# A spectral filter with a soft mixture of experts: the x step with its constant as weights, signs per row, constants in slot 4, and the read-backs of batches 1 and 2 a slot sooner

## The chip, the cores and the metric

The kernel runs on one core of a Trainium2 chip. The metric is device time in microseconds (us) of one execution, the median of the runs taken. The core's engines work side by side and wait for each other through semaphores: TensorE (PE, with the weight loads PEld beside it), VectorE (DVE), ScalarE (ACT), GpSimd (POOL), and SyncE (SP), whose queue issues most of the transfers.

## The reference

```python
X = np.fft.rfft(x, axis=1)                    # x: (8, 2496, 256)
y = np.fft.irfft(X * (filt_r + 1j * filt_i)[None], n=2496, axis=1)
x = y.reshape(19968, 256)
logits = x @ phi                              # phi: (256, 32), 8 experts of 4 slots
d = np.exp(logits - logits.max(0)); d /= d.sum(0) + 1e-09      # over the tokens
slot_input = (d.T @ x).reshape(8, 4, 256)
for e in range(8):                            # w1: (8, 256, 1024), w2: (8, 1024, 256)
    slot_out[e] = np.maximum(slot_input[e] @ w1[e], 0.0) @ w2[e]
c = np.exp(logits - logits.max(1)); c /= c.sum(1) + 1e-09      # over the 32 slots
return c @ slot_out                           # (19968, 256)
```

All of it is in float32.

## The kernel before

**The transform.** 2496 = 39 * 64, so the Fourier transform of a batch goes in two stages. The first, over 39 points, is done for batch 0 by `first_stage` (L407) and for each later batch by `s1_unit` (step s, L356, four matmuls a piece, each in a 64*64 tile of the array). It leaves 20 rows t (`NT`) of the half spectrum. The second, over 64 points, is `x_unit` (step x, L434); it takes two rows t, a pair, at a time. So a batch has ten pairs (`CPB`), and the eight batches make 80 **slots** of the main loop, slot n working on pair `divmod(n, 10)`. What batches 1 to 7 leave in the first stage, `at`, is copied out by ACT, stored in device memory (`a_dram<-at`, by `store_a`), and read back in the other order (`ash<-a_dram`, by `load_ash`); batch 0 is turned on the chip instead (`turn`).

**One slot.** `x_unit(n)` makes four products with `ash` as the weights (128 rows, 128 columns) and the constant `a1` or `b0` (128 columns) as the operand that streams. The result has the 256 channels on the partitions, in two halves. DVE multiplies it with the filter's table `ff_t`: `t2` by the imaginary part, `part` by the real one; then an addition and a subtraction give the filtered pair `yt`, on DVE in batches 0 to 5, on POOL from batch 6 on (`PA = 6`). Step t (`t_unit`, L467) works on the pair of two slots before (`LT = 2`): four transposes of 128 by 128 and a copy by ACT to `y`, where rows are on the partitions. In every second slot step l (L485), eight matmuls in 128*32 tiles with `phi_t` as the weights, makes the logits from `yt`.

**Around it.** `fold_x` (POOL) adds and subtracts two halves of a piece of x for `s1_unit`; pieces are loaded by `load_x` into six buffers (`XB = 6`), the next one as one is folded (`split_next`). `slot_of(b, u)` is the slot in which piece u of batch b is worked on; the last piece of batch 1 has slot 6, that of batch 2 slot 15. `load_to` reads a batch back no sooner than three slots behind the last piece. `chain(g)` holds the inverse transform's way back and the softmax sums for the groups (0, 1), (2, 3), (4, 5), (6), (7) of batches; its matmuls are called through `pe_m` (L515; transposes L512), in steps named ltr, v, lg, u, u2, dd, s, of which two are taken in each slot (`hop_slot`). For the last two groups the table `TAIL` says behind the slots which step follows which, by names such as `u2_5` (step u2 from row 5 on, `TG` rows at a time). Behind them come the experts (h, o) and the output blocks (out, L1087).

**The order.** SP issues its transfers in the order of the program. On PE a scheduler orders the instructions, held by `not_before` and by priorities. The list `held` keeps the instructions that are named there: `held[0]` the last of x, `held[1]` of s, `held[2]` of l. `keep_warm` (L313) runs matmuls on zeros before the first data is there; `make_signs` (L755) then spreads the signs of `sgn` over 128 partitions with 20 matmuls, and `sign_tables` multiplies the imaginary tables with them, two on DVE, the rest on POOL. The constants lie in `cst_t`; columns up to `NEAR` are loaded at the start, `NEAR:FAR` (426 KB) in slot 14.

Of the kernel before, what the change touches and what calls it, by code (L numbers as in the profile page):

```python
# [18 lines left out]
N1, N2 = 39, 64  # L19
# [46 lines left out]
TAIL = (  # L66
# [3 lines left out]
)  # L70
# [18 lines left out]
def shape_constants():  # L89
# [29 lines left out]
    def put(name, a):  # L119
        blocks.append((name, a))  # L120
# [19 lines left out]
    put("id", np.eye(P))  # L140
    put("sgn", sgn.reshape(NT // 2, P))
    put("m0", inverse(bh))
# [38 lines left out]
def filter_layout(filt):  # L181

    idx = np.array([[freq_of(t, c) for c in range(N2)] for t in range(NT)])
    a = filt[np.minimum(idx, SEQ - idx)]
    a = np.ascontiguousarray(a.reshape(NT, N2, 2, P).transpose(3, 0, 2, 1))
    return a.reshape(P, NT // 2, 256)

# [65 lines left out]
def fft_soft_moe(ctx, tc, x0, w0, x, ff, phi, wx, cst, w1q, out):  # L253
# [67 lines left out]
    eos = {}  # L321
    held = [None, None, None, None, None]

# [103 lines left out]
    def x_unit(b, c):  # L427

        t0 = 2 * c
        ash = ashs.pop((b, c))  # L430
        ps = ps_x.tile([P, 4, 2, 64], F32, tag="x", name=f"x_{b}_{c}")
        for k in range(2):
            for dh in range(2):
                ins = pe.matmul(  # L434
                    ps[:, 2 * k + dh].rearrange("q r c -> q (r c)"),
                    ash[:, k, dh * P : (dh + 1) * P],
                    C("a1" if t0 + k else "b0"),
                    start=True,
                    stop=True,
                )  # L440
# [7 lines left out]
        frv, fiv = (  # L448
            ff_t[:, c, k].rearrange("q (p o c) -> q p o c", o=1, c=64).broadcast_to([P, 4, 2, 64]) for k in range(2)
        )  # L450
        t2 = prod.tile([P, 4, 2, 64], F32, tag="t2", name=f"t2_{b}_{c}")
        if c % 2 == 0:
            yts[b, c // 2] = prod.tile([P, 2, 4, 2, 64], F32, tag="yt", name=f"yt_{b}_{c}")
        yt = yts[b, c // 2][:, c % 2]
        dve.tensor_tensor(out=t2, in0=ps[:, :, ::-1, :], in1=fiv, op=ALU.mult)  # L455
        add, part = (pool_e, yt) if b >= PA else (dve, ps)
        dve.tensor_tensor(out=part, in0=ps, in1=frv, op=ALU.mult)  # L457
        add.tensor_tensor(out=yt[:, :, 1, :], in0=part[:, :, 1, :], in1=t2[:, :, 1, :], op=ALU.add)  # L458
        add.tensor_tensor(out=yt[:, :, 0, :], in0=part[:, :, 0, :], in1=t2[:, :, 0, :], op=ALU.subtract)  # L459

    def t_unit(b, c):

        yt = yts[b, c // 2]
        pt = ps_t.tile([P, 2, 2, P], F32, tag="t", name=f"t_{b}_{c}")
        for k in range(2):
            for dh in range(2):
                pe.transpose(pt[:, k, dh, :], yt[:, c % 2, 2 * k + dh].rearrange("q r c -> q (r c)"), ident)  # L467
        k = (b * CPB + c) % YB - CPB
        if 0 <= k < CPB:
            if k == 0 and b * CPB + c < NS - CPB:  # L470
                big[0] = ypool.tile([P, CPB, 2, DIM], F32, tag="yb", name=f"yb_{b}_{c}", bufs=1)
            y = big[0][:, k]
        else:
            y = ypool.tile([P, 2, DIM], F32, tag="y", name=f"y_{b}_{c}")
        act.copy(y, pt.rearrange("k p h d -> k p (h d)"))  # L475
        ys[b, c] = y
        if c % 2 == 1:
            i = c // 2
            if i == 0:
                lts[b] = work.tile([P, 5, P], F32, tag="lt", name=f"lt_{b}", bufs=2)  # L480
            pl = ps_t.tile([P, P], F32, tag="t", name=f"l_{b}_{i}")
            with tc.high_priority():
                for dh in range(2):
                    for j in range(4):
                        ins = pe.matmul(  # L485
                            pl[32 * j : 32 * j + 32, :],
                            phi_t[:, dh, :],
                            yt[:, j // 2, 2 * (j % 2) + dh].rearrange("q r c -> q (r c)"),
                            start=(dh == 0),
                            stop=(dh == 1),  # L490
                        )
                        if j + dh == 0:
                            not_before(ins, held[1])
            held[2] = ins
            act.copy(lts[b][:, i, :], pl)  # L495

# [20 lines left out]
    def chain(g):  # L517
# [111 lines left out]
        for a0 in range(0, NH, 4):  # L629
# [21 lines left out]
            yield f"u{a0}"  # L651
        TG = SA if nb == 2 else HT // 2
        ended = [None, None]
# [38 lines left out]
        pss = psum([P, DIM], f"s_{g}")  # L692
        terms = [(ti, th, b2) for ti in range(HT) for th in range(2) for b2 in range(nb)]
        step = 4 * nb
        for k, (ti, th, b2) in enumerate(terms):
            j = k % 4
            t = th * HT + ti
            pe_m(
                pss[32 * j : 32 * j + 32, :],
                dd[:, ti, th, b2, :],  # L700
                ys[bs[b2], t // 2][:, t % 2, :],
                start=(k < 4),
                stop=(k >= len(terms) - 4),
            )
            if k % step == step - 1:
                yield f"s{k // step}"
# [40 lines left out]

    signs = []

    def make_signs(c0):  # L750
        n = min(4, NT // 2 - c0)
        ps = ps_c.tile([P, 4, 2, 1, N2], F32, tag="c", name=f"sgn_{c0}")
        for c in range(n):
            one = ident[:, c0 + c : c0 + c + 1].broadcast_to([P, P])
            behind("pe", pe.matmul(ps[:, c].rearrange("q k o c -> q (k o c)"), one, sgn_t, start=True, stop=True))  # L755
        sg = ypool.tile([P, 4, 2, 1, N2], F32, tag="y", name=f"sg_{c0}")
        act.copy(sg[:, 0:n], ps[:, 0:n])
        signs.append(sg)

    def sign_tables(c):  # L760
        if c >= CPB:
            return
        fi = ff_t[:, c, 1].rearrange("q (k h c) -> q k h c", k=2, h=2)
        sg = signs[c // 4][:, c % 4]
        (dve if c < 2 else pool_e).tensor_tensor(out=fi, in0=fi, in1=sg.broadcast_to([P, 2, 2, N2]), op=ALU.mult)

# [122 lines left out]
    for n in range(NS + LT):  # L889
        if n < NS:  # L890
            load_to(n)
            if n == CPB + 4:
                issue(cst_t[:, NEAR:FAR], cst[:, NEAR:FAR])
            if n == NS - 2 * CPB:
                behind("sp", sp.dma_start(cst_t[:, FAR:], cst[:, FAR:]))
            split_next(n + 1)
            store_a()
            x_unit(*divmod(n, CPB))
            sign_tables(n + 2)
            if n + 2 < CPB:  # L900
                turn(n + 2)
# [235 lines left out]
```

## Time and profile before

| | |
|---|---|
| Median of 3 runs | 379.02 us (378.91 to 382.27) |
| Profiled execution | 379.5 us, of which the span from its first to its last instruction is 377.7 us |
| Mean granted TensorE clock | 0.958 |
| PE, DVE, ACT, POOL busy | 350.9, 256.6, 175.4, 148.9 us |
| DMA | 103.92 MB, 275 GB/s on average |

An instruction's group in the profile is named by its line (L434 is line 434 of the kernel above), its engine, and what it writes and reads (`x<-cst_t,ash`). Behind "PE" a form such as 128*64 gives the rows and columns of the weights, and 128x256 the partitions and elements of the operand that streams. PE's timeline merges neighbours of one form into a row, with its start, its length and the number of instructions (x8). An fp32 matmul is two instructions, a transpose one. Matmuls overlap, so the length of a row is longer than the time to the next row's start.

### The profile page before, as it was taken

Reading aid. Unit: us, or ns where it says so; the run is one execution under the profiler, and the core shown is the slowest. Engines: PE = TensorE matmul, PEld = TensorE weight load, DVE = VectorE, ACT = ScalarE, POOL = GpSimd, SP = SyncE. Lnnn points to the kernel's source line nnn. Section 1 sums busy time; section 2 is a strip of 40 time slices with the busy share of each in tenths; the row PEclk is TensorE's granted clock in tenths of the full one; section 3 lists DMA queues with packets and bytes.
Section 4 is the critical chain, followed back from the end, with each engine's and each line's share of the span. In section 5 each row is a group of like instructions: output and inputs, shape, how many; then the busy total and the mean of one; then the engine's idle time right before and its main releaser. Section 6 shows DMA issues by size and latency. Waiting matters only on the chain.

```text
span 377.7 us, 10582 instructions
## 1 busy us (share of the span) xinstructions
PE 350.9 (93%) x4274; PEld 260.7 (69%) x4274; DVE 256.6 (68%) x519; ACT 175.4 (46%) x357; POOL 148.9 (39%) x180
## 2 busy tenths in 40 slices
PE   8999899699999989999999999899998999989960
PEld 6977577467677657777776787777876635878850
DVE  1576788495987987589697837766674562787540
ACT  3556545345456443545644454433363430766430
POOL 0098745453461634454253654323521302650000
PEclk9999999999999999999999999899999999999555
DMA  8999799799889685968955848333698994599996
GB/s 303 400 393 278 245 329 361 257 349 339 259 277 325 187 290 177 320 208 271 336 160 151 253 140 297 129 105 92 203 389 247 339 316 104 222 416 415 418 416 288
DMA packets 50151, 103.92 MB, mean 275 GB/s; under 512 B 5218, under 2 KB 23394, under 8 KB 47926
## 3 DMA queue, kind: packets, MB, share of 16 engines
q1 hardware_dynamic: 49412, 102.83, 78.9%
q8 instruction: 34, 0.56, 0.6%
q10 hardware_dynamic: 690, 0.42, 0.4%
q14 instruction: 15, 0.12, 0.1%
HBM read 63.11 MB, written 40.12 MB: 273 GB/s over the span
## 4 chain that ended last, share of the span: by engine, by line
PE 82%; DMA 7%; DVE 4%; ACT 2%; issue 1%; POOL 0%; DVEq 0%; ACTq 0%; SPq 0%
PE x L434 20%; PE t L467 10%; PE s L356 10%; PE l L485 6%; DMA out<-ob 5%; PE s L515 5%; PE u L515 4%; PE v L515 4%; PE s L407 3%; PE lg L515 3%; PE dd L515 2%; PE out L1087 2%; PE h L1031 2%; PE o L1049 2%; DVE ob L1092 2%; PE v L512 2%
## 5 line engine op out<-in xcount | busy, mean ns | idle before, releaser
L434 PE MATMUL x<-cst_t,ash 128*128 128x128 f32 x640 | 87.8, 280 | 6.2 <-DMA ash<-a_dram 4.1
L434 PEld LDWEIGHTS x<-cst_t,ash 128*128 128x128 f32 x640 | 78.1, 191 | 15.0 <-issue 8.3
L455 DVE TENSOR_TENSOR t<-x,ff_t 128x512 f32<-128x512 f32 x80 | 54.8, 687 | 48.6 <-PE x L434 34.2
L335 POOL TENSOR_TENSOR eo<-xt 128x512 f32<-128x512 f32 (+1 forms) x40 | 48.1, 1203 | 93.0 <-issue 89.6
L365 ACT COPY at<-s 128x1024 f32<-128x1024 f32 (+1 forms) x42 | 39.6, 942 | 48.3 <-PE s L356 34.6
L467 PE MATMUL t<-cst_t,yt 128*128 128x128 f32 x320 | 50.8, 281 | 1.5 <-POOL yt L459 1.4
L467 PEld LDWEIGHTS t<-cst_t,yt 128*128 128x128 f32 x320 | 36.2, 141 | 22.6 <-issue 9.8
L338 POOL TENSOR_TENSOR eo<-xt 128x512 f32<-128x512 f32 (+1 forms) x40 | 48.4, 1211 | 0.0
L475 ACT COPY y<-t 128x512 f32<-128x512 f32 x58 | 33.4, 589 | 24.1 <-PE t L467 22.2
L356 PE MATMUL s<-eo,w1q_t 64*64 64x512 f32 (+1 forms) x336 | 42.8, 579 | 0.0
L457 DVE TENSOR_TENSOR x<-x,ff_t 128x512 f32<-128x512 f32 x60 | 41.5, 695 | 1.2
L1087 PE MATMUL out<-so,st 32*128 32x256 f32 x468 | 35.5, 337 | 2.0 <-ACT ob L1092 1.0
L1087 PEld LDWEIGHTS out<-so,st 32*128 32x128 f32 x468 | 31.0, 222 | 5.8 <-ACT ob L1092 2.9
L1092 DVE COPY ob<-out 128x512 f32<-128x512 f32 (+1 forms) x40 | 25.0, 670 | 8.5 <-DMA out<-ob 5.8
L458 POOL TENSOR_TENSOR yt<-yt,t 128x256 f32<-128x256 f32 x20 | 15.0, 752 | 37.0 <-DVE yt L457 25.3
L1092 ACT COPY ob<-out 128x512 f32<-128x512 f32 (+1 forms) x40 | 21.7, 582 | 14.8 <-DMA out<-ob 7.9
L458 DVE TENSOR_TENSOR yt<-x,t 128x256 f32<-128x256 f32 x60 | 25.2, 420 | 1.9 <-PE l L485 0.2
L485 PE MATMUL l<-yt,phi_t 128*32 128x128 f32 x640 | 26.2, 278 | 0.0
L459 DVE TENSOR_TENSOR yt<-x,t 128x256 f32<-128x256 f32 x60 | 24.9, 414 | 0.0
L495 ACT COPY lt<-l 128x128 f32<-128x128 f32 x40 | 10.7, 268 | 30.4 <-PE l L485 30.0
L485 PEld LDWEIGHTS l<-yt,phi_t 128*32 128x32 f32 x640 | 15.4, 109 | 8.6 <-issue 5.3
L515 PE MATMUL s<-y,dd 128*32 128x256 f32 x232 | 19.3, 381 | 0.4 <-ACT dd L669 0.3
(120 smaller groups left out, 492.1 us busy)
## 6 DMA issues: line engine op xcount, KB each, us to landing
xt<-in_x SPq DMA_DIRECT2D x35, 512.0 KB
ash<-a_dram SPq DMA_DIRECT2D x70, 256.0 KB
out<-ob SPq DMA_DIRECT2D x17, 1024.0 KB
a_dram<-at SPq DMA_DIRECT2D x56, 240.0 KB
w<-in_wx SPq DMA_DIRECT2D x33, 256.0 KB
w<-in_wx SPq DMA_DIRECT2D x6, 512.0 KB
x_t<-in_x SPq DMA_DIRECT2D x5, 512.0 KB
ff_t<-in_ff SPq DMA_DIRECT2D x10, 256.0 KB
```

The source lines that it names most:

```text
L335: ins = eng.tensor_tensor(out=eo[:, 0, 0:n], in0=xs[:, :, 0], in1=xs[:, :, 1], op=ALU.add)
L338: ins = eng.tensor_tensor(out=eo[:, 1, 0:n], in0=xs[:, :, 0], in1=xs[:, :, 1], op=ALU.subtract)
L356: ins = pe.matmul(ps, w1q_t[q, c], eo[q, c, 0:n], start=True, stop=True)
L434: ins = pe.matmul(ps[:, 2 * k + dh].rearrange("q r c -> q (r c)"), ash[:, k, dh * P : (dh + 1) * P], C("a1" if t0 + k else "b0"), start=Tr ...
L455: dve.tensor_tensor(out=t2, in0=ps[:, :, ::-1, :], in1=fiv, op=ALU.mult)
L457: dve.tensor_tensor(out=part, in0=ps, in1=frv, op=ALU.mult)
L458: add.tensor_tensor(out=yt[:, :, 1, :], in0=part[:, :, 1, :], in1=t2[:, :, 1, :], op=ALU.add)
L467: pe.transpose(pt[:, k, dh, :], yt[:, c % 2, 2 * k + dh].rearrange("q r c -> q (r c)"), ident)
L485: ins = pe.matmul(pl[32 * j : 32 * j + 32, :], phi_t[:, dh, :], yt[:, j // 2, 2 * (j % 2) + dh].rearrange("q r c -> q (r c)"), start=(dh = ...
L515: line(pe.matmul(*a, **k))
L1087: nc.tensor.matmul(prs[k][:, mm, :], sts[n][q, hs, c0 : c0 + P], so[q, ho], start=(i == 0), stop=(i == 2))
L1092: copy(ob[:, nm * k : nm * (k + 1), :], prs[k])
```

## The change

Eight edits:

1. Step x takes the constant as weights, in two halves of 64 columns, and streams `ash` (256 columns). The two rows t of the pair go to the two column halves of the array. The result then has rows on the partitions and the 256 channels along them, so the filter's table is laid out that way (in `filter_layout`, on the host side of the inputs), and DVE or POOL writes `y` itself.
2. Step t transposes `y` into `yt`, which ACT copies; step l reads that copy and becomes a function of its own, `l_unit`.
3. In a slot t stands ahead of x in the program, and x is held behind t, t behind the x before (`held[5]`, `held[0]`).
4. A row's sign is now one value per partition: `make_signs` with its 20 matmuls and three copies goes, and `sign_tables` multiplies by a column of the constants.
5. In `chain`, dd has four products in 64-column tiles in place of one, its groups of rows for a single batch are six and four rows (before, five and five), the marks in `TAIL` follow, and the terms of step s are taken in another order.
6. The constants `NEAR:FAR` are issued in slot 4 in place of slot 14.
7. The read-backs of batches 1 and 2 are issued one slot sooner; loads of x pieces due in slots 6 to 8 and 15 to 17 (`quiet`) are held back until behind them; and `store_a` stands ahead of `split_next`.
8. The warm-up matmuls stream 384 columns in place of 512.

```diff
     def x_unit(b, c):
         t0 = 2 * c
         ash = ashs.pop((b, c))
-        ps = ps_x.tile([P, 4, 2, 64], F32, tag="x", name=f"x_{b}_{c}")
-        for k in range(2):
-            for dh in range(2):
+        ps = ps_x.tile([P, 2, DIM], F32, tag="x", name=f"x_{b}_{c}")
+        for r in range(2):
+            for k in range(2):
                 ins = pe.matmul(
-                    ps[:, 2 * k + dh].rearrange("q r c -> q (r c)"),
-                    ash[:, k, dh * P : (dh + 1) * P],
-                    C("a1" if t0 + k else "b0"),
+                    ps[64 * k : 64 * k + 64, r],
+                    C("a1" if t0 + k else "b0", 64 * r, 64 * r + 64),
+                    ash[:, k],
                     start=True, stop=True,
                 )
...
+                if k + r == 0:
+                    if held[5] is not None:
+                        not_before(ins, held[5])
...
         held[0] = ins
-        yt = yts[b, c // 2][:, c % 2]
-        dve.tensor_tensor(out=t2, in0=ps[:, :, ::-1, :], in1=fiv, op=ALU.mult)
-        add, part = (pool_e, yt) if b >= PA else (dve, ps)
-        dve.tensor_tensor(out=part, in0=ps, in1=frv, op=ALU.mult)
-        add.tensor_tensor(out=yt[:, :, 1, :], in0=part[:, :, 1, :], in1=t2[:, :, 1, :], op=ALU.add)
-        add.tensor_tensor(out=yt[:, :, 0, :], in0=part[:, :, 0, :], in1=t2[:, :, 0, :], op=ALU.subtract)
+        dve.tensor_tensor(out=t2, in0=ps[:, ::-1, :], in1=fiv, op=ALU.mult)
+        add, part = (pool_e, y) if b >= PA else (dve, ps)
+        dve.tensor_tensor(out=part, in0=ps, in1=frv, op=ALU.mult)
+        add.tensor_tensor(out=y[:, 1, :], in0=part[:, 1, :], in1=t2[:, 1, :], op=ALU.add)
+        add.tensor_tensor(out=y[:, 0, :], in0=part[:, 0, :], in1=t2[:, 0, :], op=ALU.subtract)
 
     def t_unit(b, c):
-                pe.transpose(pt[:, k, dh, :], yt[:, c % 2, 2 * k + dh].rearrange("q r c -> q (r c)"), ident)
+                ins = pe.transpose(pt[:, dh, r, :], ys[b, c][:, r, dh * P : (dh + 1) * P], ident)
+                if r + dh == 0:
+                    not_before(ins, held[0])
+        held[5] = ins
-        act.copy(y, pt.rearrange("k p h d -> k p (h d)"))
-        if c % 2 == 1:
+        act.copy(yts[b, c // 2][:, c % 2], pt)
+
+    def l_unit(b, c):
+        yt = yts.pop((b, c // 2))
...
                     ins = pe.matmul(
                         pl[32 * j : 32 * j + 32],
                         phi_t[:, dh, :],
                         yt[:, j // 2, dh, :, N2 * (j % 2) : N2 * (j % 2) + N2],
...
     def chain(g):
...
-        TG = SA if nb == 2 else HT // 2
+        TG = SA if nb == 2 else 6
...
-            pe_m(pd[:, 0:n], C("b1"), u2[:, t0 : t0 + n], start=True, stop=True)
+            for r in range(2):
+                for k in range(2):
+                    o = pd[64 * k : 64 * k + 64, 0 : n // 2, :, r]
+                    pe_m(o, C("b1", 64 * r, 64 * r + 64), u2[:, t0 + k : t0 + n : 2], start=True, stop=True)
...
-    def make_signs(c0):
-            behind("pe", pe.matmul(ps[:, c].rearrange("q k o c -> q (k o c)"), one, sgn_t, start=True, stop=True))
...
     def sign_tables(c):
-        (dve if c < 2 else pool_e).tensor_tensor(out=fi, in0=fi, in1=sg.broadcast_to([P, 2, 2, N2]), op=ALU.mult)
+            eng.tensor_scalar(out=fi, in0=fi, scalar1=C("sgn", c, c + 1), scalar2=None, op0=ALU.mult)
...
+    quiet = [q for b in (1, 2) for q in range(slot_of(b, NU - 1), slot_of(b, NU - 1) + 3)]
+    due = [0]
     def split_next(n):
         for b, u in at_slot.get(n, ()):
+            due[0] += 1
+            fold_x(b, u)
+        while due[0] and n - 1 not in quiet:
+            due[0] -= 1
             next_x()
-            fold_x(b, u)
...
-    keep_warm(WM)
+    keep_warm(WM, 384)
...
-            if n < max(b * CPB + c - (3 if b < 2 else ASH), slot_of(b, NU - 1) + 3):
+            if n < max(b * CPB + c - (3 if b < 2 else ASH), slot_of(b, NU - 1) + (2 if b < 3 else 3)):
...
-            if n == CPB + 4:
+            if n == 4:
                 issue(cst_t[:, NEAR:FAR], cst[:, NEAR:FAR])
...
+            store_a()
             split_next(n + 1)
-            store_a()
+        if n >= LT:
+            t_unit(*divmod(n - LT, CPB))
+        if n < NS:
             x_unit(*divmod(n, CPB))
...
         if n >= LT:
             b, c = divmod(n - LT, CPB)
-            t_unit(b, c)
+            if c % 2 == 1:
+                l_unit(b, c)
```

**On PE, at the end of batch 1 and the start of batch 2 (in x_8, x_9, x_0 the number is the pair of the batch; s_3_2 is piece 2 of batch 3), the order before:**

```order
L467 MATMUL t_6_946<-cst_t,yt_6_864 128x128 x4
L434 MATMUL x_9_961<-cst_t,ash_9_852 128x128 x4
L467 MATMUL t_7_971<-cst_t,yt_6_864 128x128 x4
L512 MATMUL ltr_0_1065<-cst_t,lt_767 128x128
L434 MATMUL x_0_994<-cst_t,ash_0_916 128x128 x4
L485 MATMUL l_3_977<-yt_6_864,phi_t 32x128 x8
L356 MATMUL s_3_2_1005<-eo_2_956,w1q_t 64x512 x4
L467 MATMUL t_8_1012<-cst_t,yt_8_934 128x128 x4
L512 MATMUL ltr_0_1065<-cst_t,lt_767 128x128
L434 MATMUL x_1_1022<-cst_t,ash_1_918 128x128 x4
L467 MATMUL t_9_1039<-cst_t,yt_8_934 128x128 x4
L434 MATMUL x_2_1083<-cst_t,ash_2_920 128x128 x4
```

The same place after the change (`yb_0` is the tile that holds a whole batch of y; x's weights are now 64 columns of `cst_t`, with `ash` streaming 256):

```order
L471 MATMUL t_6_909<-cst_t,yb_0_650 128x128 x4
L432 MATMUL x_8_915<-ash_8_790,cst_t 64x256 x4
L354 MATMUL s_3_1_925<-eo_1_873,w1q_t 64x512 x4
L514 MATMUL ltr_0_1047<-cst_t,lt_748 128x128
L471 MATMUL t_7_941<-cst_t,yb_0_650 128x128
L487 MATMUL l_3_957<-yt_6_908,phi_t 32x128 x2
L471 MATMUL t_7_941<-cst_t,yb_0_650 128x128 x3
L432 MATMUL x_9_947<-ash_9_830,cst_t 64x256 x4
L487 MATMUL l_3_957<-yt_6_908,phi_t 32x128 x6
L471 MATMUL t_8_975<-cst_t,yb_0_650 128x128 x4
L432 MATMUL x_0_981<-ash_0_861,cst_t 64x256 x4
L354 MATMUL s_3_2_992<-eo_2_936,w1q_t 64x512 x4
```

A t step stands where x stood between two others, and each x step is now of another form than the t steps around it. The l step, which was one piece of eight, stands in a piece of two in the middle of a t step and a piece of six behind the next x.

**On SP's queue, where batch 1 is read back (`a_dram<-at` stores a piece, `ash<-a_dram` reads a pair back, `xt<-in_x` loads a piece of x), the order before:**

```order
L307 DMA xt_0_533<-in_x 128x512
L307 DMA a_dram_262<-at_5_524 60x3x256 x2
L307 DMA a_dram_262<-at_5_524 20x256 x2
L307 DMA a_dram_560<-at_0_566 60x2x256 x2
L307 DMA ash_0_612<-a_dram_262 128x512
L307 DMA ash_1_614<-a_dram_262 128x512
L307 DMA ash_2_616<-a_dram_262 128x512
L307 DMA xt_1_618<-in_x 128x1024
L307 DMA a_dram_560<-at_1_603 60x4x256 x2
L307 DMA ash_3_652<-a_dram_262 128x512
```

The same place after the change:

```order
L305 DMA a_dram_243<-at_5_512 60x3x256 x2
L305 DMA a_dram_243<-at_5_512 20x256 x2
L305 DMA ash_0_564<-a_dram_243 128x512
L305 DMA ash_1_566<-a_dram_243 128x512
L305 DMA a_dram_546<-at_0_552 60x2x256 x2
L305 DMA ash_2_595<-a_dram_243 128x512
L305 DMA a_dram_546<-at_1_593 60x4x256 x2
L305 DMA xt_5_602<-in_x 128x1024
L305 DMA xt_0_604<-in_x 128x512
L305 DMA xt_1_606<-in_x 128x1024
```

The read-backs `ash_0` and `ash_1` now stand directly behind the last store of batch 1 (`at_5`), ahead of the first store of batch 2 (`at_0`), and three loads of x pieces stand behind the third read-back.

More of the change, by code (lines that the diff above doesn't have):

```diff
@@ L140, in shape_constants @@
     put("id", np.eye(P))
-    put("sgn", sgn.reshape(NT // 2, P))
+    put("sgn", sgn.reshape(NT // 2, P).T)
     put("m0", inverse(bh))
@@ L184, in filter_layout @@
     a = filt[np.minimum(idx, SEQ - idx)]
[L185 to L186 removed]
+    return np.ascontiguousarray(a.reshape(NT // 2, P, DIM).transpose(1, 0, 2))
 def weight_layout(w1, w2):
@@ L321, in fft_soft_moe @@
     eos = {}
-    held = [None, None, None, None, None]
+    held = [None] * 6
     def not_before(ins, other):
@@ L447, in x_unit @@
         held[0] = ins
[L448 to L453, printed above, removed]
-        yt = yts[b, c // 2][:, c % 2]
-        dve.tensor_tensor(out=t2, in0=ps[:, :, ::-1, :], in1=fiv, op=ALU.mult)
-        add, part = (pool_e, yt) if b >= PA else (dve, ps)
[L457 to L467, printed above, removed]
+        frv, fiv = (ff_t[:, c, k].rearrange("q (o d) -> q o d", o=1).broadcast_to([P, 2, DIM]) for k in range(2))
+        t2 = prod.tile([P, 2, DIM], F32, tag="t2", name=f"t2_{b}_{c}")
         k = (b * CPB + c) % YB - CPB
@@ L474, in t_unit @@
             y = ypool.tile([P, 2, DIM], F32, tag="y", name=f"y_{b}_{c}")
-        act.copy(y, pt.rearrange("k p h d -> k p (h d)"))
-        ys[b, c] = y
-        if c % 2 == 1:
[L478 to L495, printed above, removed]
+        dve.tensor_tensor(out=t2, in0=ps[:, ::-1, :], in1=fiv, op=ALU.mult)
@@ new lines, in x_unit, with t_unit @@
+        add, part = (pool_e, y) if b >= PA else (dve, ps)
+        dve.tensor_tensor(out=part, in0=ps, in1=frv, op=ALU.mult)
+        add.tensor_tensor(out=y[:, 1, :], in0=part[:, 1, :], in1=t2[:, 1, :], op=ALU.add)
+        add.tensor_tensor(out=y[:, 0, :], in0=part[:, 0, :], in1=t2[:, 0, :], op=ALU.subtract)
+        ys[b, c] = y
+    def t_unit(b, c):
+        if c % 2 == 0:
+            yts[b, c // 2] = prod.tile([P, 2, 2, 2, P], F32, tag="yt", name=f"yt_{b}_{c}")
+        pt = ps_t.tile([P, 2, 2, P], F32, tag="t", name=f"t_{b}_{c}")
+        for r in range(2):
+            for dh in range(2):
+                ins = pe.transpose(pt[:, dh, r, :], ys[b, c][:, r, dh * P : (dh + 1) * P], ident)
[3 more added lines that the diff above has]
+        act.copy(yts[b, c // 2][:, c % 2], pt)
@@ new lines, in l_unit @@
+    def l_unit(b, c):
+        yt = yts.pop((b, c // 2))
+        i = c // 2
+        if i == 0:
+            lts[b] = work.tile([P, 5, P], F32, tag="lt", name=f"lt_{b}", bufs=2)
+        pl = ps_t.tile([P, 2, N2], F32, tag="t", name=f"l_{b}_{i}")
+        with tc.high_priority():
+            for dh in range(2):
+                for j in range(4):
+                    ins = pe.matmul(
+                        pl[32 * j : 32 * j + 32],
+                        phi_t[:, dh, :],
+                        yt[:, j // 2, dh, :, N2 * (j % 2) : N2 * (j % 2) + N2],
+                        start=(dh == 0),
+                        stop=(dh == 1),
+                    )
+                    if j + dh == 0:
+                        not_before(ins, held[1])
+        held[2] = ins
+        act.copy(lts[b][:, i, :], pl.rearrange("q r c -> q (r c)"))
@@ L664, in chain @@
             n = min(TG, HT - t0)
-            pd = psum([P, TG, 2, nb, SLOTS], f"dd_{g}_{t0}")
-            pe_m(pd[:, 0:n], C("b1"), u2[:, t0 : t0 + n], start=True, stop=True)
-            if t0 == 0:
-                pe_m(pd[:, 0, 0], C("bh"), u2[:, 0, 0], start=True, stop=True)
-            ended[0] = act.copy(dd[:, t0 : t0 + n], pd[:, 0:n])
+            pd = psum([P, TG // 2, 2, 2, nb, SLOTS], f"dd_{g}_{t0}")
+            for r in range(2):
+                for k in range(2):
+                    o = pd[64 * k : 64 * k + 64, 0 : n // 2, :, r]
+                    pe_m(o, C("b1", 64 * r, 64 * r + 64), u2[:, t0 + k : t0 + n : 2], start=True, stop=True)
+                if t0 == 0:
+                    pe_m(pd[0:64, 0, 0, r], C("bh", 64 * r, 64 * r + 64), u2[:, 0, 0], start=True, stop=True)
+            ddv = dd.rearrange("q (h l) r b e -> q l h (r b e)", h=2)
+            ended[0] = act.copy(
+                ddv[:, t0 // 2 : (t0 + n) // 2], pd[:, 0 : n // 2].rearrange("q l h r b e -> q l h (r b e)")
+            )
             if t0 != 0:
@@ L692, in chain @@
         pss = psum([P, DIM], f"s_{g}")
-        terms = [(ti, th, b2) for ti in range(HT) for th in range(2) for b2 in range(nb)]
+        terms = [(c, r, b2) for c in range(HT) for r in range(2) for b2 in range(nb)]
         step = 4 * nb
-        for k, (ti, th, b2) in enumerate(terms):
+        for k, (c, r, b2) in enumerate(terms):
             j = k % 4
-            t = th * HT + ti
             pe_m(
                 pss[32 * j : 32 * j + 32, :],
-                dd[:, ti, th, b2, :],
-                ys[bs[b2], t // 2][:, t % 2, :],
+                dd[:, c, r, b2, :],
+                ys[bs[b2], c][:, r, :],
                 start=(k < 4),
@@ L746, in load_tables @@
         issue(ff_t[:, c], ff[:, c])
-    signs = []
-    def make_signs(c0):
[L751 to L758, printed above, removed]
-    def sign_tables(c):
[L761 to L764, printed above, removed]
-        (dve if c < 2 else pool_e).tensor_tensor(out=fi, in0=fi, in1=sg.broadcast_to([P, 2, 2, N2]), op=ALU.mult)
+    def sign_tables(c):
+        if c < CPB:
+            fi = ff_t[:, c, 1]
+            eng = dve if c < 2 else pool_e
+            eng.tensor_scalar(out=fi, in0=fi, scalar1=C("sgn", c, c + 1), scalar2=None, op0=ALU.mult)
     NS = BATCH * CPB
```

4 lines of the change are left out of this document (removed), and 4 rows, old and new, of the table TAIL.

## Prediction

> **What bounds the kernel now.** I read the page first: busy time, then the chain of work that ended last.
>
> ```profile
> span 377.7 us, 10582 instructions
> ...
> PE 350.9 (93%) x4274; PEld 260.7 (69%) x4274; DVE 256.6 (68%) x519; ACT 175.4 (46%) x357; POOL 148.9 (39%) x180
> ...
> PE 82%; DMA 7%; DVE 4%; ACT 2%; issue 1%; POOL 0%; DVEq 0%; ACTq 0%; SPq 0%
> ```
>
> TensorE (PE) is busy 93% and carries 82% of the chain. The windows view then tells the stages apart; the first number behind the comma is PE's busy time.
>
> ```profile
> 23.00:273.00 250.00, 242.21 (x2901) 177.80 (x2900) 190.52 (x368) 120.85 (x226) 121.98 (x121) 0.99 0.76 247
> 240.50:244.00 3.50, 3.50 (x54) 3.17 (x56) 3.19 (x8) 2.24 (x6) 1.27 (x2) 0.51 0.14 51
> ```
>
> In the 250 us of the slots PE works 242 us, DVE 191. The time is PE's own instruction stream there, plus its waits. The waits view lists those (total, times, longest):
>
> ```profile
> PE x L434 <- DMA ash<-a_dram: 4.1, 2, 2.5
> PE t L467 <- POOL yt L459: 1.4, 1, 1.4
> PE x L434 <- issue: 1.1, 1, 1.1
> PE x L434 <- DVE yt L459: 1.0, 1, 1.0
> ```
>
> So the change is judged by what it does to PE's stream, and by which of these 7.6 us it removes. The second window adds one thing: the granted clock was 0.51 for 3.5 us just after the 1.4 us wait, which cost PE about 1.7 us.
>
> **What a step costs on PE.** Read starts, not durations: a step costs the start of the next minus its own. Behind the line number stand the weights' rows*columns; 128*64 means that two matmuls run beside each other, one in each half of the array's columns, 128*32 four.
>
> ```profile
> 84.41 0.33 PE L512 MATMUL ltr<-cst_t,lt 128*128 128x128 f32 x1
> 84.67 1.04 PE L515 MATMUL v<-cst_t,lsb 128*64 128x66 f32 x28
> 85.64 0.33 PE L467 MATMUL t<-cst_t,yt 128*128 128x128 f32 x1
> 85.90 0.64 PE L485 MATMUL l<-yt,phi_t 128*32 128x128 f32 x16
> 86.47 0.33 PE L467 MATMUL t<-cst_t,yt 128*128 128x128 f32 x1
> ...
> 87.70 0.44 PE L467 MATMUL t<-cst_t,yt 128*128 128x128 f32 x2
> 88.07 0.92 PE L515 MATMUL v<-cst_t,lsb 128*64 128x66 f32 x24
> 88.92 1.16 PE L434 MATMUL x<-cst_t,ash 128*128 128x128 f32 x8
> 89.92 0.60 PE L467 MATMUL t<-cst_t,yt 128*128 128x128 f32 x4
> 90.35 1.06 PE L434 MATMUL x<-cst_t,ash 128*128 128x128 f32 x8
> 91.34 0.66 PE L356 MATMUL s<-eo,w1q_t 64*64 64x512 f32 x4
> ...
> 103.75 1.06 PE L434 MATMUL x<-cst_t,ash 128*128 128x128 f32 x8
> 104.64 0.60 PE L467 MATMUL t<-cst_t,yt 128*128 128x128 f32 x4
> 105.08 1.06 PE L434 MATMUL x<-cst_t,ash 128*128 128x128 f32 x8
> ```
>
> Each fp32 product is two MATMULs, a transpose one. Between t steps an x step costs 0.89 us (103.75 to 104.64), a t step 0.44: 0.11 per matmul, x after t or t after x free. But x before s, a 64*64 step, costs 0.99 (90.35 to 91.34), and x after v costs 1.00 before t. A lone t matmul between v and l costs 0.26. v shows it as well: 28 matmuls take 0.97 us and 24 take 0.85, so a pair takes 0.06, fourteen pairs 0.83, and 0.14 is left. **Each change of the array's shape costs about 0.15 us**, 0.10 before the first matmul of the new shape and 0.03 to 0.10 behind it, where its second weights load in the open. The Trainium skill, TensorEngine Tiling (Array Packing), Key Properties, has a rule that speaks against this change: changing the tiling mode drains the engine. The trace agrees (0.44 for t alone, 0.26 for a quarter of it between shapes); the page gives no price, so a sum by it alone could be anything from here up.
>
> For the new x step I need 256 columns in two tiles. The nearest rows are those of the chain step s, four tiles, on both sides of an l of the same shape:
>
> ```profile
> 201.63 1.69 PE L515 MATMUL s<-y,dd 128*32 128x256 f32 x28
> 203.14 0.62 PE L485 MATMUL l<-yt,phi_t 128*32 128x128 f32 x16
> 203.58 1.48 PE L515 MATMUL s<-y,dd 128*32 128x256 f32 x24
> 204.99 1.16 PE L434 MATMUL x<-cst_t,ash 128*128 128x128 f32 x8
> ```
>
> 28 matmuls, seven rounds of four, take 1.51 us: 0.216 a round. l takes 0.44 where the shape stays and 0.57 between t matmuls (85.90 to 86.47).
>
> **The change part by part.**
>
> *x step.* Before eight matmuls of 0.11, 0.89 us; now eight of 256 columns in pairs, four rounds of 0.216, 0.86 us. 80 steps save 2.4 us. The Trainium skill, TensorE: Matmul & The Clock Gate, LDWEIGHTS, says that a weight load takes its columns over 1.2 ns; if loads bounded x, 64 columns for 128 would halve it. The s rows, whose weights have 32 columns, still take 0.216 a round, so the columns that stream set the pace.
>
> *Shape changes.* The new x is a 128*64 step among 128*128 transposes. Counted in the two instruction orders up to the first output matmul, PE changes its shape 216 times before and 377 times now: entries into x 26 then, 84 now; into t 40 and 75; into l 37 and 63; into ltr 4 and 29; dd 2 and 11; lg 2 and 8. 161 more at 0.15 are **+24 us**. From both sides: 0.10 (nothing but the first gap) gives 16, 0.20 (x after v against x between t: 0.11 behind the change, 0.10 before it) gives 32. I take 0.15, what v, l and t show. The new dd stands in this count; its columns stay the same, as its pairs run beside each other.
>
> *Pieces.* l now waits for ACT's copy of t, and the new order issues 28 of the 40 l steps as two matmuls of the program and then six, with t, x or others between; 8 x steps are cut as 1 and 3. A cut l uses two of the four tiles, then all: six rounds of 0.11 for four, 0.22 more; a cut x six rounds of 0.216 for four, 0.43 more. The chain shows the price of such a rest:
>
> ```profile
> 140.26 1.84 PE s L515 x26
> ...
> 203.76 1.29 PE s L515 x24
> ```
>
> Two matmuls more cost 0.55 us where the 26 began with the fourth tile alone. So 28 x 0.22 + 8 x 0.43 = 9.6, less some 1.5 for cuts of that kind which the old order had: **+8**. Bounds: 0 if the rest of the array fills in, 10.
>
> *Signs and warm-up.*
>
> ```profile
> 1.45 3.74 PE warm_up L313 x4
> 5.19 6.25 PE s L407 x56
> 11.44 0.90 PE sgn L755 x8
> ...
> 14.12 0.90 PE sgn L755 x8
> ```
>
> Twenty sign matmuls go: 0.90 twice and half of it once, 2.2 us, on the path since x starts after them. ACT's copies of them were beside it. The sign multiply by a scalar has no row; the old one on POOL lies two slots ahead of its x, so 0 to 1 us more each is hidden, and if not, it would hold the first slots by up to 1 us. The warm-up loses a quarter of 3.7, 0.9, but the first s matmuls then run at the half clock until about 5 us: -0.5. Together **-2.7**.
>
> *Read-backs.*
>
> ```profile
> 39.91 4.15 SPq L307 DMA_DIRECT2D a_dram<-at  x6
> 44.73 1.29 SPq L307 DMA_DIRECT2D ash<-a_dram  x3
> ...
> 47.62 2.23 PE L434 MATMUL x<-cst_t,ash 128*128 128x128 f32 x16 [1.60 <-DMA ash<-a_dram]
> ```
>
> The read-back of batch 1 was issued behind the next batch's first store and landed 2.9 us later. Now it is issued ahead of that store, some 1.4 us sooner, and PE has 1.4 us more to do between. Batch 2 likewise: -4.1 us, both ends 0 and -4.1. The pieces of x held back are loaded up to six ahead, so three slots of some 3 us cover them; uncovered, a fold would wait some 3 us for one. The constants that move to slot 4 meet no read-back there; before slot 30 nothing reads them.
>
> *Other waits.* A slower PE meets DVE's and the 'issue' waits (2.1) less: -2.1. The wait on POOL stays in part, -0.7; the clock dip followed it, -1.7. All four can stay: 0. New ones: t(n-2) now stands behind x(n-1), not behind x(n), so DVE must finish within a t, an x and mostly an s or l: 0.6 + 1.0 + 0.6 to 1.0.
>
> ```profile
> L455 DVE TENSOR_TENSOR t<-x,ff_t 128x512 f32<-128x512 f32 x80 | 54.8, 687 | 48.6 <-PE x L434 34.2
> L457 DVE TENSOR_TENSOR x<-x,ff_t 128x512 f32<-128x512 f32 x60 | 41.5, 695 | 1.2
> L458 DVE TENSOR_TENSOR yt<-x,t 128x256 f32<-128x256 f32 x60 | 25.2, 420 | 1.9 <-PE l L485 0.2
> L458 POOL TENSOR_TENSOR yt<-yt,t 128x256 f32<-128x256 f32 x20 | 15.0, 752 | 37.0 <-DVE yt L457 25.3
> ```
>
> DVE needs 0.69 + 0.70 + twice 0.42 = 2.2: covered. In batches 6 and 7 POOL adds twice 0.75 instead: 2.9, short by up to 0.7 in 20 units. Queued behind such a t is x(n), and DVE behind that. Bounds 0 and 8; I take 0, since the old trace has one such wait.
>
> **Sum.** 24 + 8 - 2.4 - 2.7 = +27 on PE; waits -4.1 - 2.1 - 0.7 - 1.7 = -8.6. The profiled execution took 379.5 us (1.8 beyond its span, 0.5 above the median of 379.0): 379.5 + 18.4 = **398 us**. The output stage behind it, DMA and PE, only moves along.
>
> **The rivals.**
> - Cut steps cost nothing: the idle tiles are filled by what follows. Then +8 falls away: 390. Against it stands the 0.55 above. 0.14.
> - New waits: POOL, or l behind ACT's copies, take 8 us: 406. DVE and ACT have slack (76% and 48% of the slots), against it. 0.07.
> - It does not do what it says: the read-backs still come late, +4: 402. 0.05.
> - The other side: the shape price is one of late weights, and x's constant weights are loaded ahead of it. It decides when entry into x and back is free: 24 us fall away, the cuts fill in, and 26 old entries are gone (-5): 379.5 - 5 - 5 - 8.6 = 361. Against it: s and l have constant weights too (w1q_t, phi_t) and pay. 0.03.
> - The page's load rule: x were bound by loads and halves, 80 x 0.43 = 34 us less: 364. The s rows speak against it. 0.02.
> - Small prices (0.10) with all waits gone and the cuts free: 379.5 + 16 - 5 - 9 = 382, within 1%. 0.02.
>
> My forecast has 0.67. The range takes in 390 and 406 and a shape price of 0.13: 387 to 406. A measurement of this kernel tells 1% from no change. Faster 0.05, same 0.02, slower 0.93.
>
> **What would show it.** Right: x between t steps costs 1.0 us from start to start and a t step 0.6 in place of 0.44; l in two pieces; no wait on ash at the starts of batches 1 and 2; PE near 95% busy and the first output matmul near 341 us (323 before). Wrong: x to t in 0.9 us, or waits of more than 8 us on POOL or ACT in the slots. What would overturn it is the order on the chip giving cheap x entries.

## The result and the profile after

The changed kernel takes **400.6 us** (median; 400.35 to 400.94), 1.0547 times the kernel before (95% interval 1.0504 to 1.059). Here and below a ratio compares the fast runs of a kernel with those of the kernel before, measured beside it (379.6 us here, 380.1 to 380.7 below), while a median takes in every run. Forecast were 398 us and a range of 387 to 406. The page of the changed kernel, busy time first and then the chain's engines:

```profile
span 398.9 us, 10674 instructions
...
PE 375.3 (94%) x4342; PEld 227.3 (57%) x4342; DVE 263.7 (66%) x519; ACT 176.9 (44%) x354; POOL 150.6 (38%) x180
...
PE 73%; DMA 10%; DVE 6%; POOL 3%; ACT 2%; issue 1%; SPq 1%; ACTq 0%; DVEq 0%; POOLq 0%
```

PE is busy for 24 us more, with 68 instructions more; DVE for 7, ACT and POOL for 2 or less. PE's share of the chain fell, from 82% to 73%, though it waits less: the chain now runs through SP's queue and the transfers ahead of a late read-back, and counts time in which PE was at work. So the idle time is the better measure here. Now the windows view over the stretch that the change touches, from the first x matmul to the first output matmul, of the kernel before and then of the changed one.

```profile
19.06:322.58 303.52, 293.32 (x3641) 210.94 (x3638) 218.12 (x441) 141.00 (x280) 135.87 (x147) 0.99 0.77 253
```
```profile
17.16:343.55 326.39, 320.08 (x3728) 179.51 (x3725) 225.52 (x441) 143.98 (x280) 138.44 (x147) 1.00 0.73 237
```

The whole result stands in these two rows. The stretch starts 1.9 us earlier (signs and warm-up), lasts 22.9 us longer and ends 21.0 us later; the span grew by 21.2. Of the 303.5 us before, PE was idle for 10.2 and lost 1.7 to the clock (3.4 us at half clock near 240.5), so its stream is 291.6 us. Of the 326.4 us after, it is idle for 6.3, with the clock at 1.00: 320.1 us. So **PE's stream grew by 28.5 us, and its waits with the clock shrank by 5.6**. The waits view of the changed kernel says which are left:

```profile
PE x L432 <- DMA ash<-a_dram: 1.5, 1, 1.5
...
PE l L487 <- ACT yt L475: 1.0, 1, 1.0
PE t L471 <- DVE yb L461: 0.9, 1, 0.9
...
PE t L471 <- POOL y L461: 0.4, 1, 0.4
```

The stream's growth can be read off PE's timeline, from start to start:

```profile
45.59 0.64 PE L487 MATMUL l<-yt,phi_t 128*32 128x128 f32 x16
46.17 0.66 PE L471 MATMUL t<-cst_t,y 128*128 128x128 f32 x4
46.75 1.08 PE L432 MATMUL x<-ash,cst_t 128*64 128x256 f32 x8
47.77 1.09 PE L354 MATMUL s<-eo,w1q_t 64*64 64x512 f32 x8
...
108.57 0.41 PE L487 MATMUL l<-yt,phi_t 128*32 128x128 f32 x4
108.92 0.27 PE L514 MATMUL mt<-cst_t,cmax 117*32 117x117 f32 x1
109.12 0.63 PE L487 MATMUL l<-yt,phi_t 128*32 128x128 f32 x12
109.68 0.66 PE L471 MATMUL t<-cst_t,y 128*128 128x128 f32 x4
110.27 1.08 PE L432 MATMUL x<-ash,cst_t 128*64 128x256 f32 x8
```

Before x, t takes 0.58 us (46.17 to 46.75; 0.44 before the change), and x takes 1.02 (before the change 0.89 between two t, 0.99 ahead of an s step). The l step comes in a piece of 0.35 and one of 0.56, where a whole one takes 0.58 (45.59 to 46.17).

### The profile page after: what moved, and what is told of

Same layout as the page of the kernel before. It is cut to its first block, busy times and chain, and to the rows that moved or that the text cites. A ratio compares the mean times of both kernels' runs of the same rounds, so it can differ in the third digit from the quotient of the medians.

```text
span 398.9 us, 10674 instructions
## 1 busy us (share of the span) xinstructions
PE 375.3 (94%) x4342; PEld 227.3 (57%) x4342; DVE 263.7 (66%) x519; ACT 176.9 (44%) x354; POOL 150.6 (38%) x180
## 4 chain that ended last, share of the span: by engine, by line
PE 73%; DMA 10%; DVE 6%; POOL 3%; ACT 2%; issue 1%; SPq 1%; ACTq 0%; DVEq 0%; POOLq 0%
PE x L432 19%; PE t L471 10%; PE s L354 9%; PE l L487 7%; DMA out<-ob 5%; PE s L517 5%; PE u L517 3%; PE v L517 3%; PE dd L517 3%; PE lg L517 3%; DMA phi_t<-in_phi 2%; PE ltr L514 2%; PE h L1033 2%; PE o L1051 2%; DVE ob L1094 2%; DMA ash<-a_dram 2%
## 5 line engine op out<-in xcount | busy, mean ns | idle before, releaser
L432 PE MATMUL x<-ash,cst_t 128*64 128x256 f32 x640 | 91.3, 392 | 1.5 <-DMA ash<-a_dram 1.5
L475 ACT COPY yt<-t 128x512 f32<-128x512 f32 x80 | 46.9, 586 | 36.5 <-PE t L471 35.3
L432 PEld LDWEIGHTS x<-ash,cst_t 128*64 128x64 f32 x640 | 39.9, 136 | 28.1 <-issue 12.6
L471 PE MATMUL t<-cst_t,y 128*128 128x128 f32 x232 | 39.5, 286 | 0.4 <-POOL y L461 0.4
L487 PE MATMUL l<-yt,phi_t 128*32 128x128 f32 x640 | 36.9, 281 | 1.0 <-ACT yt L475 1.0
L487 PEld LDWEIGHTS l<-yt,phi_t 128*32 128x32 f32 x640 | 18.8, 108 | 25.2 <-issue 16.1
L471 PEld LDWEIGHTS t<-cst_t,y 128*128 128x128 f32 x232 | 25.2, 141 | 13.9 <-issue 10.5
L460 POOL TENSOR_TENSOR y<-y,t 128x256 f32<-128x256 f32 x18 | 13.1, 728 | 40.5 <-DVE y L459 38.3
L460 DVE TENSOR_TENSOR y<-x,t 128x256 f32<-128x256 f32 x40 | 16.8, 421 | 1.6 <-PE s L517 0.6
L354 PEld LDWEIGHTS s<-eo,w1q_t 64*64 64x64 f32 x336 | 8.8, 131 | 14.9 <-issue 13.6
```

Of the source, the lines that this page charges most:

```text
L354: ins = pe.matmul(ps, w1q_t[q, c], eo[q, c, 0:n], start=True, stop=True)
L432: ins = pe.matmul(ps[64 * k : 64 * k + 64, r], C("a1" if t0 + k else "b0", 64 * r, 64 * r + 64), ash[:, k], start=True, stop=True,)
L471: ins = pe.transpose(pt[:, dh, r, :], ys[b, c][:, r, dh * P : (dh + 1) * P], ident)
L475: act.copy(yts[b, c // 2][:, c % 2], pt)
L487: ins = pe.matmul(pl[32 * j : 32 * j + 32], phi_t[:, dh, :], yt[:, j // 2, dh, :, N2 * (j % 2) : N2 * (j % 2) + N2], start=(dh == 0), stop ...
```

## The experiments

Two theories stood against each other: that the array's changes of shape lengthen PE's stream, or that the new order and its waits do. A third question was what the moved transfers are worth.

**The shape alone, in the kernel before.**

```diff
-                    ps[:, 2 * k + dh].rearrange("q r c -> q (r c)"),
-                    ash[:, k, dh * P : (dh + 1) * P],
...
+                for e in range(2):
+                    lo = dh * P + 64 * e
...
+                        ps[64 * e : 64 * e + 64, 2 * k + dh].rearrange("q r c -> q (r c)"),
+                        ash[:, k, lo : lo + 64],
```

> The kernel before with one thing changed: each product of step x is split into two of 64 weight columns, side by side in the two halves of the array. Result, layout, order of t, l and all transfers stay. The stream that passes is as long as before (eight matmuls of 128 columns in pairs), but x is now of another shape than t: in the instruction order PE changes its shape 355 times before the first output, 216 in the kernel before. Theory (each change costs about 0.15 us, cut steps leave half the array idle): 139 x 0.15 = 21 us, 4 us more for x steps cut at odd counts, less 2 us of waits on DVE that a slower PE no longer meets: 402 us, at least 396. Rival (the loss of the changed kernel comes from its new waits and its order, the shape costs nothing): 379 to 383 us. Rival (loads of 128 weight columns bound x, halves are cheaper): below 375 us.

Measured: 399.3 us, ratio 1.0519 (1.0452 to 1.0586). Only the products of x changed (twice as many, half as wide), and nearly the whole loss of the changed kernel is there.

```profile
20.20:340.52 320.32, 314.93 (x4280) 206.04 (x4276) 223.13 (x441) 142.26 (x280) 136.50 (x146) 1.00 0.74 238
```

PE's stream is 314.9 us, 23.3 above the 291.6 of the kernel before. Counted in the two traces, it has 141 changes more (369 for 228). With the 4 us that were set aside for cut steps, an estimate, this gives 0.14 us a change; if those steps cost nothing, 0.165. PE's idle time fell from 10.2 to 5.4 us here too: a slower PE meets fewer waits, and no part of the change is needed for that.

**The shape taken out of the changed kernel.**

```diff
-            for k in range(2):
-                    ps[64 * k : 64 * k + 64, r],
-                    C("a1" if t0 + k else "b0", 64 * r, 64 * r + 64),
-                    ash[:, k],
+            for k in range(1):
...
+                    ps[:, r],
+                    C("a1" if t0 + r else "b0"),
+                    ash[:, r],
```

> The changed kernel, but step x runs as two full-array matmuls of 256 columns (128 weight columns) in place of four half-array ones in pairs. The stream is as long, the constants still are the weights and ash streams; rows land in other places, so the values of x are not the reference's. Order of t, x, l and all waits stay. Shape changes in the order: 272, 377 in the changed kernel. Theory: 105 changes less at 0.15 us are 16 us, and 2.5 us for x steps that can no longer leave half the array idle: 382 us, 380 to 386. Rival (new waits or order): within 3 us of the changed kernel's 400.6.

Measured: 385.5 us, ratio 1.0147 (1.0092 to 1.0202), 15 us below the changed kernel.

```profile
96.04 1.03 PE L432 MATMUL x<-ash,cst_t 128*128 128x256 f32 x4
96.91 1.02 PE L517 MATMUL lg<-v,cst_t 120*117 120x512 f32 x2
...
99.81 0.66 PE L471 MATMUL t<-cst_t,y 128*128 128x128 f32 x4
100.30 1.03 PE L432 MATMUL x<-ash,cst_t 128*128 128x256 f32 x4
101.26 1.09 PE L354 MATMUL s<-eo,w1q_t 64*64 64x512 f32 x8
```
```profile
17.37:328.66 311.29, 303.07 (x3409) 193.52 (x3405) 223.75 (x441) 144.33 (x280) 139.37 (x147) 0.99 0.76 248
```

A t step that the array enters from l still takes 0.49, but x behind it is entered for nothing: 0.96 with the change to s, and 0.87 where the next step (lg, 120*117) takes the whole array too. Against 1.02 with a change on both sides that is 0.15 us, read off the rows alone. The stream is 303.1 us, 1.7 of it a stretch at half clock, so 18.7 less than 320.1, for 107 changes (282 for 389 in the traces) and 8 cut x steps: 0.15 us a change, if those steps cost the 2.5 us expected (0.175 if they cost nothing). Program order and transfers were those of the changed kernel, and PE was idle for 8.2 us, 6.3 in the changed kernel, so the gain doesn't come from waits: that rival falls for this part.

**The l step in one piece.**

```diff
-                for j in range(4):
+                for j in (2, 3, 0, 1):
...
-                    if j + dh == 0:
+                    if (j, dh) == (2, 0):
```

> The changed kernel with l's eight matmuls in another order: the two that read the later pair come first, so l can't start until ACT has copied that pair, and is no longer cut into two and six. Shape changes 338, 377 in the changed kernel; all 40 l steps whole. Theory (a cut l costs 0.22 us of idle tiles and a shape change more): 28 x 0.22 = 6 us and 39 x 0.14 = 5 us less, 390 us, 388 to 393. Rival (what follows fills the idle tiles): only the shape changes, 395 us. Rival (l whole waits for ACT's copy instead): 400 us or more.

Measured: 394.5 us, ratio 1.0388 (1.033 to 1.0445): 6 us gained, not 10.

```profile
17.29:338.11 320.82, 312.38 (x3728) 178.47 (x3724) 224.83 (x441) 143.40 (x280) 138.75 (x147) 0.99 0.74 241
```
```profile
PE x L432 <- DMA ash<-a_dram: 2.2, 1, 2.2
PE l L487 <- ACT yt L475: 1.5, 1, 1.5
...
PE t L471 <- DVE yb L461: 1.5, 1, 1.5
...
PE ltr L514 <- ACT lt L497: 1.2, 3, 0.4
```

The stream, less 1.7 of half clock, is 310.7 us: 9.4 gained. But PE is idle for 8.4 us, 6.3 in the changed kernel: x behind its read-back, l behind ACT, t behind DVE and ltr behind ACT each wait 0.5 to 0.8 us more. So the time lies between theory and rival. 41 changes (348 for 389) at 0.15 are 6.2 us, which leaves 3.2 for 28 cut steps, 0.11 each where 0.22 was expected. The rows of the changed kernel divide the gain otherwise: pieces of 0.35 and 0.56 us for a whole l of 0.58 are 0.33 more a cut, 9.2 us for 28. Taken off this, the 0.22 for two more rounds on half the tiles leaves 0.11 for the further change. What a cut costs is shown; how much of it is idle tiles is not.

**The transfers undone in the changed kernel, and done alone in the kernel before.** Both edits are the same lines, taken out of the one and put into the other: `quiet` and `due`, the 2 or 3 in `load_to`, slot 4 or 14, and the place of `store_a`.

> The changed kernel with the transfers as in the kernel before: read-backs of batches 1 and 2 a slot later, pieces of x loaded when due, constants in slot 14, the store behind the load. The prediction gave these moves -4.1 us. Theory: PE again waits for the read-back at the starts of batches 1 and 2, 404 us (402 to 405). Rival (the slower PE hides the read-backs anyway): 400 to 401 us, no wait on ash over 0.5 us.

> The kernel before with the transfers of the changed one alone: read-backs of batches 1 and 2 a slot sooner, pieces of x held back, constants in slot 4, the store ahead of the load. There PE waits 4.1 us for the read-backs at the starts of batches 1 and 2, with x ahead of t in the slot. Theory now (the moves take these waits away where x is at PE's door early, as it is here, but the burst of three pieces of x holds the fourth read-back back by 1.5 to 2 us, as in the changed kernel at 57 us): 377 us. Rival (the full 4.1 us): 375.5. Rival (the waits only move, as the undone moves in the changed kernel changed nothing): 379 to 380.

Measured: undone 400.1 us, ratio 1.0542 (1.0495 to 1.059), as the changed kernel; done alone 379.4, ratio 1.0009 (0.9975 to 1.0043), as the kernel before. So the moves gain nothing in either (in the kernel before the interval leaves about 1 us of the 4.1), and the rivals hold. Where the 4.1 us stayed is seen in the kernel before with the moves, first in the windows row, then on SP's queue and in PE's waits:

```profile
20.18:322.23 302.05, 291.61 (x3641) 209.43 (x3637) 217.95 (x441) 140.77 (x280) 135.51 (x146) 1.00 0.77 253
```
```profile
41.01 1.81 SPq L307 DMA_DIRECT2D a_dram<-at  x4
46.23 0.82 SPq L307 DMA_DIRECT2D ash<-a_dram  x2
47.09 0.94 SPq L307 DMA_DIRECT2D a_dram<-at  x2
48.07 0.44 SPq L307 DMA_DIRECT2D ash<-a_dram  x1
48.55 0.97 SPq L307 DMA_DIRECT2D a_dram<-at  x2
49.56 2.42 SPq L307 DMA_DIRECT2D xt<-in_x  x2
```
```profile
SPq L307 <- DMA a_dram<-at: 3.2, 2, 3.0
```
```profile
48.92 2.02 PE L434 MATMUL x<-cst_t,ash 128*128 128x128 f32 x16 [1.80 <-DMA ash<-a_dram]
58.86 2.05 PE L434 MATMUL x<-cst_t,ash 128*128 128x128 f32 x16 [2.13 <-DMA ash<-a_dram]
```

The read-back now stands right behind its own batch's last stores in the queue, but it is issued 5.2 us after the first of them, where it was 4.8 before the change (39.91 to 44.73). The third fence is SP's waits from 41.6 to 46.4 us: 3.2 of them for these stores to land. Before the change the next batch's store stood in that gap and cost nothing. So PE still waits 1.80 us, and 2.13 more for the fourth read-back, ahead of which loads of x pieces now stand in a row. With 1.29 at the start of batch 2 (2.47 before; PE comes there later now) and 0.35 for another, its waits on ash are 5.6 us, 1.5 more than before. The stream is 291.6 us as before. This execution began x 1.1 us later but lost nothing to the clock (1.7 before), and the wait of 1.0 us on DVE is gone; so its time comes out the same.

**No piece of x held back, in the changed kernel.**

```diff
-    quiet = [q for b in (1, 2) for q in range(slot_of(b, NU - 1), slot_of(b, NU - 1) + 3)]
+    quiet = []
```

> The changed kernel with no load of a piece of x held back; read-backs and constants as they are. One piece (512 KB) then stands ahead of the first read-back of batch 1, and one, not three, ahead of the fourth. Theory (the three loads in a row are what the fourth read-back waits behind): the wait of 1.5 us on ash near 57 us is gone, that near 47 us at most 0.5 us, time 399 to 400. Rival (the fourth read-back is late for its own reason, such as its store): the wait near 57 us stays at over 1 us.

Measured: 402.8 us (400.2 to 406.5), ratio 1.0582 (1.0499 to 1.0665), which doesn't tell it from the changed kernel; the trace does. First the changed kernel's row for the fourth read-back, then the only such wait without the holding back:

```profile
56.98 1.08 PE L432 MATMUL x<-ash,cst_t 128*64 128x256 f32 x8 [1.55 <-DMA ash<-a_dram]
```
```profile
48.64 1.08 PE L432 MATMUL x<-ash,cst_t 128*64 128x256 f32 x8 [1.58 <-DMA ash<-a_dram]
```

The wait at 57 us goes, as the theory has it, but one of the same size stands at the first read-back, where at most 0.5 was expected. Holding the pieces back only moves a wait by three slots.

**Two slots' steps together.** In the changed kernel (with l in one piece), and in the kernel before (there with the shorter warm-up, once with the transfers moved and with l's later pair first, and once without either, as shown here). The last line of the edit reads the later batches back one slot less ahead, in all three:

```diff
-            x_unit(*divmod(n, CPB))
+            if n % 2 == 1:
+                x_unit(*divmod(n - 1, CPB))
+                x_unit(*divmod(n, CPB))
...
-            t_unit(b, c)
+            if n % 2 == 1:
+                t_unit(*divmod(n - 1 - LT, CPB))
+                t_unit(*divmod(n - LT, CPB))
...
-            if n < max(b * CPB + c - (3 if b < 2 else ASH), ...
+            if n < max(b * CPB + c - (3 if b < 2 else ASH - 1), ...
```

> The changed kernel with l's later pair first and two slots' steps together: x, x, t, t in every second slot in place of t, x in each, so that PE changes its shape 258 times before the first output, 377 in the changed kernel, 338 with l's order alone. Same products, and the read-backs of batches from 2 on one slot less ahead. Theory (a change costs 0.13 to 0.15 us): 119 changes less are 16 to 18 us and the whole l and x steps some 7 us, less up to 5 us that come back as waits on ACT and DVE: 379 us, 375 to 383. Rival (a waiting chain of x, DVE and t bounds the slots): no faster than the 394.5 of l's order alone.

> The kernel before with the transfers of the changed one, its shorter warm-up and two slots' steps together (x, x, t, t). x and t have one shape there, so this saves only 8 changes against the kernel with the transfers alone. Theory: 1 us for those, 1 us for x steps in one piece, 0.5 us for the warm-up: 2 us less than the kernel with the transfers alone, 375 us. Rival (the paired order makes t wait for DVE, or x for its two result banks): 380 us or more.

> The kernel before with the steps of two slots together (x, x, t, t) and the shorter warm-up, and its own transfers: no read-back sooner, no piece held back, constants in slot 14. PE's order has 207 shape changes before the first output, 216 in the kernel before. Theory (the transfers as moved give nothing, the gain of the kernel with both, 0.9937 of before, is all from the pairs and the warm-up): ratio 0.990 to 0.996, 375 to 378 us. Rival (the pairs gain only with the read-backs sooner): 379 us or more, ratio 0.998 to 1.005.

Measured: changed kernel 382.8 us, ratio 1.0082 (1.0056 to 1.0109); kernel before with the transfers 377.5, ratio 0.9937 (0.9906 to 0.9967); without them 377.0, ratio **0.9919** (0.9886 to 0.9951), the lowest here, though its interval overlaps the other's. In the paired order two more turn and two more s steps come ahead of the first x, so the next rows begin at the first turn step: the kernel before, the changed one with l's order alone, and the pairs.

```profile
17.45:322.58 305.13, 294.93 (x3653) 212.01 (x3654) 219.20 (x443) 142.13 (x282) 136.75 (x147) 0.99 0.77 253
```
```profile
15.69:338.11 322.42, 313.98 (x3740) 179.53 (x3740) 226.18 (x444) 144.31 (x281) 139.44 (x147) 0.99 0.74 242
```
```profile
15.26:325.65 310.39, 298.23 (x3741) 179.28 (x3742) 222.54 (x444) 141.78 (x281) 138.67 (x147) 1.00 0.76 252
```
```profile
PE l L487 <- ACT yt L475: 3.9, 5, 1.6
PE u L517 <- ACT d L624: 1.9, 1, 1.9
```

With the same products as the changed kernel, but 270 changes for 389, the stream is 298.2 us, 5 above the 293.2 of the kernel before (294.9 less 1.7 of half clock). Against l's order alone (312.3 without its 1.7 of half clock) it gains 14 us; the 78 changes less give 11.7 at 0.15, and the rest was not taken apart. Both edits to the shape of x had changed the number of matmul instructions too; here it stays (x3740 and x3741), so it is not their number that costs. PE is idle for 12.2 us now, 3.9 of it at l: what the transposed copy costs once the shape no longer hides it. In the kernel before, pairing with the shorter warm-up gains 0.6% with the moved transfers and 0.8% without; how much of that the warm-up gives was not tried.

## Why the prediction was right, and where it was off

- **Shape changes (+24).** Right in mechanism and size. Two experiments with opposite edits give 0.14 and 0.15 us a change with the estimates for cut steps, 0.165 and 0.175 with none, and the rows of t and x 0.14 and 0.15; 161 at 0.15 were taken. The Trainium skill, TensorEngine Tiling (Array Packing), Key Properties, says that a change of tiling mode drains the engine; the runs agree that each change costs time, and put the price at about 0.15 us.
- **Step x (-2.4) and cut steps (+8).** The stream grew by 28.5 us; 24 + 8 - 2.4 made 29.6. At 0.15 a change a cut l leaves tiles idle for 0.11, not 0.22, and then the +8 was nearer 5; by the rows of l it is 0.22, and a change of l costs 0.11. So the sum holds to 1.1 us, while the division between these two terms stays open. The x step by itself was sized rightly (0.87 in the run without the change of shape). The weight loads did get shorter (PEld is busy for 227.3 us, 260.7 before), and x did not: 1.02 us where 0.89 stood. By the rule of the Trainium skill, TensorE: Matmul & The Clock Gate, LDWEIGHTS, that a load takes as many ns as it has columns, divided by 1.2, x would have halved if loads bounded it; the trace shows that they don't.
- **Signs and warm-up (-2.7).** 1.9: the first x starts at 17.16 us, 19.06 before. This start moves by about 1 us with the moment at which the clock becomes whole (5.0 and 5.3 us in these two); where that was 7.3 us, x began at 18.00 with the changed opening (transfers undone) and at 20.16 with the old one (transfers alone), 2.2 apart.
- **Read-backs (-4.1).** This step failed. PE's waits on ash did fall, from 4.1 to 1.5 us, but they fall without the moves as well (PE comes to the first x of batch 1 at 47.7 us, where it came at 46.0; the row of the changed kernel with the transfers undone is below). So 2.6 us of this term came out by luck. The prediction read SP's rows as a queue in which the next store held the read-back up. It is the landing of the batch's own stores that holds it.

```profile
47.86 1.08 PE L432 MATMUL x<-ash,cst_t 128*64 128x256 f32 x8 [0.19 <-DMA ash<-a_dram]
```

- **Other waits (-4.5).** The waits on DVE and on issue went, that on POOL fell from 1.4 to 0.4, and the clock stayed whole at 240 us. New are 1.0 us behind ACT and 0.9 behind DVE. In all the waits gave 5.6 us, not 8.6: 3.0 less. The opening gave 0.8 less, and the stream grew by 1.1 less than forecast; together that is the difference between forecast (398) and result.
- **The rivals.** "It does not do what it says" described the read-backs truly, but not their price: the waits went for another reason. Of what was to be seen, the t step (0.58), the x step (1.0), l in pieces, no wait on ash at the starts of batches 1 and 2, and PE at 94% came out; the first output matmul came at 343.6 us, not 341.

## What to carry to other kernels

Where TensorE bounds a kernel, count how often the shape of the array changes from one step to the next, and price each change from start-to-start times in the kernel's own timeline (about 0.15 us here); a step that becomes cheaper by itself can lose more than it gains if its neighbours have another shape. Steps of one shape put next to each other win much of it back (14 us of PE's stream here, 11.7 us of the time), and even a kernel whose main steps share a shape gained 0.8% from the same grouping with a shorter warm-up. A transfer that waits for an earlier one to land gains little by an earlier place in the queue: look at what the queue's engine waits for before moving it.

## What the hardware showed

The granted clock falls to about half for some 3.4 us in four of the eleven kernels profiled here and not in the others: at 240.5 us in the kernel before, behind a wait of 1.4 us on POOL; at 237.7 us in the kernel before with pairs and transfers, behind 1.7 on POOL; at 57.3 us in the changed kernel with the whole shape, behind 1.9 on ash; and at 57.2 us in the changed kernel with l in one piece, behind its wait of 2.2 us on ash. The windows row of the last, and then the kernel before with the transfers moved, which has the same wait on POOL and kept its clock there:

```profile
57.20:60.60 3.40, 3.40 (x28) 1.85 (x26) 2.15 (x4) 0.85 (x2) 0.00 (x0) 0.50 1.03 397
```
```profile
241.80:245.30 3.50, 3.49 (x76) 3.26 (x76) 3.32 (x8) 2.81 (x9) 1.15 (x2) 1.00 0.18 62
```
```profile
PE t L467 <- POOL yt L459: 1.4, 1, 1.4
```

Behind the longest wait of the kernel before, 2.47 us at 74 us, there was no dip either. The clock record of the traces shows more: in all four the dip lasts 3.41 us and begins a whole number of such intervals after the clock became whole (69 in the kernel before, 235.52 us; 68 and twice 15 in the others), and the wait lies within the interval just ahead of it. The wait at 74 us was cut in two by the border of an interval, 1.02 and 1.45 us. So where a wait falls seems to have a part in it, and that shifts with the start of the clock. It doesn't settle it: an interval with 1.79 us of idle time had no dip behind it (the kernel before with the transfers moved, at 55.1 us), one with 1.37 had. So the 1.7 us that the prediction tied to a wait come and go, and which waits bring them stays open.
